# Fourier mixing and channel mix on one core: later row tables made by TensorE from the first, the sigmoid table loaded in the opening, slot 0's fold on VectorE

## The chip, the core and the metric

The kernel runs on one core of one Trainium2 chip. Five engines work from their own instruction queues: PE (TensorE, matrix products; PEld is its weight load), DVE (VectorE), ACT (ScalarE), POOL (GpSimd) and SP (SyncE, which here only issues transfers). They wait for each other by semaphores. The metric is the device time of one execution in microseconds (us), lower is better.

## The reference

The input x has 8 batches of 3072 rows and 256 columns. A two-dimensional Fourier transform is taken of each batch and its real part kept; the result goes through a channel mix with a gate:

```python
X = np.fft.fft(np.fft.fft(x, axis=1), axis=2).real
x_prev = X shifted down by one row (first row zero)
xk = mu_k * X + (1 - mu_k) * x_prev
xr = mu_r * X + (1 - mu_r) * x_prev
k = np.maximum(xk @ w_k, 0.0)          # 256 -> 1024
v = k * k @ w_v                        # 1024 -> 256
r = 1 / (1 + np.exp(-(xr @ w_r)))      # 256 -> 256
out = r * v
```

## The kernel before

**The transform in stages.** 3072 is 48 times 64, and only the real part is wanted. Each batch goes through these stages:

- *Fold* (`fold`, L171 and L173, DVE): rows of x (`xp`) plus the mirrored rows (`xm`, gathered by POOL) give `p`. A batch has two halves h, of nine and eight *slots* q. For batch 0 the folds come in parts, as the loads arrive; slot 0 of half 0 alone is folded by POOL (`fold(0, 0, 0, 1, nc.gpsimd)` within `loads`).
- *Stage A* (products with cosine and sine tables over the 48 rows, from `p` or from its sums and differences `eo`, which `butterfly` makes). Batch 0 uses `a_sum` (L592), batch 1 `a_item`, both with the table `w_pm`. Batches 2 to 7 (`a_half`, L551, and `a_slot_0`, L548) have their rows in another order: two groups of 48 rows begin at partitions 0 and 64, of 112 in all, and use the tables `w_h` and `w_h0`. `w_h0` is for slot 0 alone.
- *Stage D* (`d_units`, L614) multiplies by the tables `w_eo`, and gives `g_all`; `turned` (L637) rotates one column of each unit by a product with the table `turn`.
- *Stage C* (`c_sums`, `c_pairs`, L655) multiplies by `m_cs`; ACT and DVE evacuate the result to `y`.
- `diff`, `mix` and `mix_part` (DVE) make xk and xr from `y`.

**The channel mix.** A *chunk* is 512 rows of the output, six to a batch, 48 in all. A chunk takes four *steps*; the k products of a step (`k_products`, L766) go to a PSUM buffer of two banks, ACT makes the relu of it (L776, `rl`) and DVE the square (L786, `k`; in steps 7, 8 and 9 ACT, L784). The r products of a chunk (`r_item`, L793) go through ACT's sigmoid (L798). The v products (`v_part`, L819, in the first chunks, later `v_tile`, L807) follow some steps behind, and DVE multiplies v and r (`v_out`, L829) for the store on SP's queue.

**PSUM.** There are three buffers `psW` of two banks and two `psV` of one bank, taken in turn in the order of the program. So a product can wait for the evacuation of what lay in its buffer before.

**The tables.** In the opening the angles are products of small rows on PE; DVE wraps them, and ACT takes their sine (`w_pm` L386 and L388, `m_cs` L443, `w_eo` L487). The angles of `w_h` and `w_h0` are made by POOL (`half_rows`, L494 to L501), wrapped by DVE in step 3 (`half_tables`, L265 on `u_h`), taken through three sines by ACT (L508, L512) and scaled by DVE in step 8 (`half_scale`). The sine is in one table of functions of ACT and the sigmoid in another. ACT_TABLE_LOAD, which the compiler puts in where the function asks for it, stands ahead of the first sine (L262) and of the first sigmoid (L798, in step 5).

**The order.** All engines run in the order in which the program text issues (`pin_order`). After the opening, a loop over steps issues the k products, then the work that `at` and `event` have put down for the step: kind "x" (products with their evacuation) ahead of the step's v products, "e" (events) behind them, "w" (DVE's work) last, and then the square. In the opening, products without use (`keep_busy`, L206) fill PE's waits; `NF` holds their numbers.

**The queues.** POOL issues the loads of x, the gathers and the weights; SP issues the first load of x, the two rows of mu (L221) and all stores but three, which ACT issues at the end. The loads of batch 1 wait for a `gate` (a write by DVE, then one by POOL, L464 and L465). ACT copies mu's rows into `mu_p` (`mu_rows`, L226), which PE turns into columns (L851, `muf_t`). `zero_rows` (L423, DVE, step 3) clears rows 48 to 63 of two load buffers, which batch 2 and later don't load. `eo_rest` writes two single columns of `w_eo`, `m_first` (L450) clears one column of `m_cs`.

Of the kernel before, what the change touches and what calls it, by code (L numbers as in the profile page):

```python
# [9 lines left out]
FP32 = mybir.dt.float32  # L10
# [10 lines left out]
def _v(ap, extra_offset, free_dims):  # L21
    new_ap = [list(ap.ap[0])] + [[s, c] for (s, c) in free_dims]
    return dataclasses.replace(ap, offset=ap.offset + extra_offset, ap=new_ap)
# [16 lines left out]
def kernel(  # L40
# [98 lines left out]
    def gather(dst, src, idx):  # L139
        nc.gpsimd.indirect_dma_start(dst, None, src, bass.IndirectOffsetOnAxis(ap=idx, axis=0))  # L140
# [15 lines left out]
            load_m0(b)  # L156
        load_m(b, h, 0, 8, (idx_g8 if b > 1 else idx_8)[:, b, h:h + 1])

    def fold(b, h, q0=0, n=0, eng=None):

        n, eng = n or 9 - h, eng or V
        if (b, h) not in p_t:
            p_t[b, h] = p_pool.tile([112, 9, 256], FP16, name="p")
        k = parts(b)
        p, xp, xm = p_t[b, h][0:k], xp_t[b, h][0:k], xm_t[b, h][0:k]
        o = XM0 + 256 * (8 - h - q0)
        if (b, h, q0) == (0, 0, 0):
            xm, o = xm_00, 1
        if (b, h) == (0, 0) and q0 < 5:
            xp = xp_32  # L170
        eng.tensor_tensor(out=p[:, q0:q0 + n], in0=xp[:, q0:q0 + n],  # L171
                          in1=_v(xm, o + 256, [(-256, n), (-1, 256)]), op=ALU.add)
        eng.tensor_tensor(out=p[:, q0:q0 + n, 0], in0=xp[:, q0:q0 + n, 0],  # L173
                          in1=_v(xm, o, [(-256, n)]), op=ALU.add)

    def butterfly(b, h, n=0):
# [31 lines left out]

    fill = ps_w()
    keep_busy(4, fill)  # L210
    NF = (8, 2, 1, 3, 0, 3, 0)

# [3 lines left out]
    mu_p = const.tile([2, 2, P], FP32)  # L218
    unit = const.tile([2, 2], FP32)
    for i, mu in enumerate((moe_mu_k, moe_mu_r)):  # L220
        nc.sync.dma_start(out=mu_row[i:i + 1], in_=mu.rearrange("(a b) -> a b", a=1))  # L221

    def mu_rows(a):
        for p0, f0, step, n in (((0, 0, 1, 1), (1, 2, 2, 63), (64, 1, 2, 64)),
                                ((0, 128, 1, 1), (1, 254, -2, 63), (64, 255, -2, 64)))[a]:
            nc.scalar.activation(out=mu_p[:, a, p0:p0 + n], in_=_v(mu_row, f0, [(step, n)]),  # L226
                                 func=AF.Copy)
# [35 lines left out]
    def ts(out, in0, s1, op0, s2=None, op1=None):  # L263
        kw = {} if op1 is None else {"op1": op1}
        V.tensor_scalar(out=out, in0=in0, scalar1=s1, scalar2=s2, op0=op0, **kw)  # L265
# [46 lines left out]
    for i in range(2):  # L312
        nc.scalar.activation(out=unit[:, i:i + 1], in_=g_i[0:2], func=AF.Copy, bias=1.0 - i,
                             scale=2.0 * i - 1.0)

    ts(rv(JR, 0, (1, P)), one, 0.0, ADD)
    ts(rv(PN, 0, (2, 64), (1, 2)), _v(one, 0, [(2, 64), (0, 2)]), 0.0, ADD)
# [21 lines left out]
    WA, WB = 4 * NU, 2 * NU  # L339
    u_w = const.tile([P, 3, NU], INT32)  # L340
    w_pm = const.tile([P, 3, WA + WB], FP16)
    u_h = const.tile([P, 3, NU], INT32)
    w_h = const.tile([112, WB], FP16)
    w_h0 = const.tile([112, WB], FP16)
    u_p = const.tile([P, 2], INT32)
    u_c = const.tile([P, 2], FP32)
    u_j = const.tile([P, NU], INT32)
    ph_c = const.tile([P, 4], FP32)
    ang = (k2_pool.tile([P, 8, 512], FP16, name="rl", tag="rl")
           .rearrange("p a b -> p (a b)").bitcast(INT32)[:, 0:2 * NJ * 64]  # L350
# [37 lines left out]
        nc.scalar.activation(out=_v(w_pm, WA + g, [(WA + WB, 2), (2, NU)]),  # L388
                             in_=_v(u_w, 2 * NU, [(0, 2), (1, NU)]), **kw)

    mu_rows(0)
    mu_rows(1)

    def wrap_angles(j0, j1):
        ts(ang[:, :, j0:j1], ang[:, :, j0:j1], TURN - 1, ALU.bitwise_and)

# [23 lines left out]

    def zero_rows():
        for n in (0, 2):
            V.memset(xp_sb[n][32:64, 8], 0.0)  # L423

    def mirrored_mu():

# [4 lines left out]
    def turn_table():  # L431
        ts(turn, ramp, cols[:, 0:1], ALU.is_equal, cols[:, 1:2], MUL)
# [9 lines left out]
    def m_sine(j0, j1):  # L442
        nc.scalar.activation(out=m_cs[:, 0:2, j0:j1], in_=ang[:, :, j0:j1], func=AF.Sin,  # L443
                             bias=m_pi, scale=TWO_PI / TURN)
# [2 lines left out]
        ts(m_cs[:, 2], m_cs[:, 1], -1.0, MUL)  # L447

    def m_first():
        V.memset(_v(m_cs[hi64], 0, [(NJ * 64, 2)]), 0.0)  # L450

    def loads():
        rows()
        for a in range(2):
            gather(wk_sb[0][a], moe_w_k, row_i[:, a:a + 1])
        fold(0, 0, 0, 1, nc.gpsimd)
        nc.gpsimd.dma_start(out=wv_sb, in_=moe_w_v.rearrange("(fc p) v -> p fc v", p=128))
        half_rows()

# [13 lines left out]
    def loads_2():  # L473
        for lo in (0, 64):
            k = slice(lo, 64 if lo == 0 else 112)
            iota(idx_g8[k], pattern=[[S // 8, B], [-1, 2]], base=S // 8 - 1 - lo // 16,
                 channel_multiplier=-8)
            iota(idx_g0[k], pattern=[[S, B]], base=S - lo // 2, channel_multiplier=-64)
        iota(idx_g0[0:1], pattern=[[S, B]], base=0, channel_multiplier=0)
        for a in range(2):  # L480
            gather(wk_sb[1][a], moe_w_k, row_i[:, 2 + a:3 + a])
        load_xh(1, 1)
        for a in range(2):
            gather(wr_sb[1][a], moe_w_r, row_i[:, 2 + a:3 + a])

    def eo_sine():
        nc.scalar.activation(out=w_eo.rearrange("p a b -> p (a b)"),  # L487
# [2 lines left out]


    def half_rows():
        G = nc.gpsimd
        iota(u_j, pattern=[[1, NU]], base=0, channel_multiplier=0)  # L494
        for lo in (0, 64):
            for k in range(2):
                iota(u_p[lo:lo + 64, k:k + 1], pattern=[[0, 1]], base=k * lo // 64,
                     channel_multiplier=2)
        G.tensor_scalar(out=u_c, in0=u_p, scalar1=TURN / 96.0, scalar2=None, op0=MUL)
        for n, (k, ph) in enumerate(((0, 0.75), (0, 0.5), (1, 0.625))):  # L500
            G.tensor_scalar(out=u_h[:, n], in0=u_j, scalar1=u_c[:, k:k + 1], scalar2=ph * TURN,  # L501
                            op0=MUL, op1=ADD)

    def half_tables():
        ts(u_h, u_h, TURN - 1, ALU.bitwise_and)
        V.memset(w_h0, 0.0)
        kw = dict(func=AF.Sin, scale=TWO_PI / TURN)
        nc.scalar.activation(out=_v(w_h, 0, [(1, 2), (2, NU)]), in_=u_h[0:112, 0:2],  # L508
                             bias=m_pi[0:112], **kw)
        for g in range(2):  # L510
            rows = slice(64 * g, 64 * g + N1)
            nc.scalar.activation(out=_v(w_h0[rows], g, [(2, NU)]), in_=u_h[rows, 2],  # L512
                                 bias=m_pi[rows], **kw)
    def half_scale():
        ts(w_h0, w_h0, math.sqrt(0.5), MUL)

    def eo_rest():

        ts(w_eo[:, 0, 0:1], g_i, -1.0, MUL, 1.0, ADD)
        ts(w_eo[:, 0, 64:65], g_i, 0.0, ADD)  # L520


    a_t = {}
# [3 lines left out]
    def evac(out_ap, in_ap, eng):  # L527
        if eng == "V":
            V.tensor_copy(out=out_ap, in_=in_ap)
        else:  # L530
            nc.scalar.activation(out=out_ap, in_=in_ap, func=AF.Copy)  # L531
# [48 lines left out]
    def a_sum(b, h, i0, eng="A", m=4):  # L580


        if (h, i0) == (0, 0):
            a_tile(b)
        ps = ps_w() if m == 4 else ps_v()
        for i in range(m):
            parts = [(h, i0 + i + 1 - h, 0, 2 * WA, 0, 1)]
            if h and i0 + i == 7:
                parts = [(0, 0, 0, WA, WA, 1), (1, 7, 1, WA, 1, 2)]
            for half, q, o, n, w, step in parts:  # L590
                for k in range(2):
                    nc.tensor.matmul(out=_v(ps, 256 * i + o, [(2 * WA // n, n)]),  # L592
                                     lhsT=p_t[b, half][0:96, q, 128 * k:128 * k + 128],
                                     rhs=_v(w_pm[0:96], (WA + WB) * k + w,
                                            [(WA + WB, 2), (step, n // 2)]),
                                     start=(k == 0), stop=(k == 1))
        a_ps[b, h, i0] = ps
        if eng:
            a_evac(b, h, i0, eng, m)
# [34 lines left out]
    def turned(u0, u1, ps=None, eng="A"):  # L634
        ps = ps_w() if ps is None else ps
        f128 = _v(g_all, 256 * u0 + 128, [(256, u1 - u0)])
        nc.tensor.matmul(out=ps[:, 0:u1 - u0], lhsT=turn, rhs=f128, start=True, stop=True)  # L637
        evac(f128, ps[:, 0:u1 - u0], eng)

# [203 lines left out]
    m_sine(0, NJ1)  # L845
    eo_sine()
    m_sine(NJ1, NJ)
    fold(0, 0, 1, 4)
    mu_ps = ps_v()
    for a in range(2):  # L850
# [11 lines left out]
    fold(0, 1, 0, 4)  # L862
    a_sum(0, 1, 0, "A")
    fold(0, 1, 4, 4)
    eo_rest()
    m_first()
    turn_table()
    a_sum(0, 1, 4, "V", 2)
    a_sum(0, 1, 6, "A", 2)
    nc.scalar.activation(out=mu_n, in_=mu_f, func=AF.Copy, bias=1.0, scale=-1.0)  # L870
    m_neg()
    fill = ps_w()
# [51 lines left out]
    def at(step, f, *args):  # L924
        work.setdefault((step, "x" if f in (a_item, a_sum, d_item, d_small, c_item, c_tiles, turned, minus_0, r_item) else "w"),
                        []).append((f, args))
# [39 lines left out]
    at(0, diff, 0, 0, 4)  # L966
    at(1, d_small, 0, 12, 1)
    at(2, mix_part, 0, 1, 0, 8)
    at(3, zero_rows)
    event(3, (turned, 8, 13))  # L970
    event(4, (c_item, 0, 17, 8))
    at(4, loads_2)
    at(4, fold, 1, 0)
# [5 lines left out]
    at(7, butterfly, 1, 0, 1)  # L979
    at(7, diff, 0, 24, 26)  # L980
    at(7, mix_part, 0, 1, 8, 16)
    at(3, half_tables)
    at(8, half_scale)
    at(8, mix, 0, 0, 1, 0)
    at(9, r_item, (0, 0, 1))
    at(9, mix, 0, 0, 1, 1)
# [147 lines left out]
```

## Time and profile before

| | us |
|---|---|
| median of 3 runs | 433.0 (432.94 to 434.78) |
| the profiled execution's own time | 432.96 |
| its span, first to last instruction | 431.2 |
| PE busy in the span | 423.2 |
| DVE busy | 361.4 |
| ACT busy | 321.1 |
| POOL busy | 63.2 |

The profile is one execution with times from the span's start. "Busy" for PE is modelled and includes pipelined overlap. A timeline row gives start, length, engine, line, operation, what is written and read, and the number of instructions merged into it; brackets hold the idle time of the engine before it, and what released it. The chain is followed back from the last instruction: at each step to what released it.

### The profile page before, as it was taken

The page shows a single profiled execution, that of the slowest core. Times are in us where ns is not written, and L with a number is a line of the kernel's source. Part 1 is how long each engine was busy: PE and PEld are TensorE (multiplying, and loading weights), DVE is VectorE, ACT ScalarE, POOL GpSimd, SP SyncE. Part 2 cuts the span into 40 slices and gives each one's busy share as a digit, 9 for nine tenths or more (in the row PEclk, how much of TensorE's full clock was granted, in tenths as well). Part 3 has the DMA queues.
Part 4 walks back from the last instruction along what each step waited for, and adds up shares of the span by engine and source line. Part 5 has one row for each costly group of instructions (what it writes and reads, how often), then busy time and mean ns, then how long its engine had stood idle before and what let it go on. Part 6 is the DMA issues. An engine that isn't in the chain of part 4 may idle for free.

```text
span 431.2 us, 9311 instructions
## 1 busy us (share of the span) xinstructions
PE 423.2 (98%) x3853; PEld 298.2 (69%) x3853; DVE 361.4 (84%) x552; ACT 321.1 (74%) x375; POOL 63.2 (15%) x100
## 2 busy tenths in 40 slices
PE   8999999999999999999999999999999999999996
PEld 3656776777767776777677777777676766766765
DVE  8899989997998979988898988989799847997453
ACT  7799798877778678777877777777786867666661
POOL 7785402000050001400041000500000000000000
PEclk9999999999999999999999999999999999999999
DMA  8999926323286223943259223772232322223233
GB/s 170 137 150 208 220 54 111 82 60 75 52 145 152 69 69 62 184 104 75 49 106 192 70 50 74 131 162 63 62 75 49 75 62 63 65 65 72 69 74 98
DMA packets 35102, 42.06 MB, mean 98 GB/s; under 512 B 4114, under 2 KB 31092, under 8 KB 35060
## 3 DMA queue, kind: packets, MB, share of 16 engines
q1 hardware_dynamic: 27492, 25.41, 23.8%
q0 software_dynamic: 7264, 15.80, 22.3%
q8 instruction: 30, 0.49, 0.5%
q10 hardware_dynamic: 304, 0.26, 0.2%
q14 instruction: 12, 0.10, 0.1%
HBM read 32.08 MB, written 25.17 MB: 133 GB/s over the span
## 4 chain that ended last, share of the span: by engine, by line
PE 93%; DVE 5%; ACT 1%; issue 0%; POOL 0%; ACTq 0%
PE psW L766 38%; PE psV L807 36%; PE psW L793 10%; PE psW L614 2%; PE psV L819 2%; PE psW L687 1%; PE psW L574 1%; DVE p L171 1%; DVE rl L265 1%; PE psW L655 1%; ACT rl L776 0%; DVE k L786 0%; PE psW L592 0%; DVE x L731 0%; DVE d L708 0%
## 5 line engine op out<-in xcount | busy, mean ns | idle before, releaser
L776 ACT ACTIVATE rl<-psW 128x1024 f16<-128x1024 f32 x192 | 195.2, 1025 | 91.1 <-PE psW L766 87.4
L766 PE MATMUL psW<-x,wk 128*128 128x512 f16 (+1 forms) x776 | 195.7, 377 | 0.7 <-ACT r L798 0.2
L807 PE MATMUL psV<-wv_sb,k 128*128 128x256 f16 x1424 | 184.1, 273 | 0.0
L807 PEld LDWEIGHTS <-k 128*128 128x128 f16 x1424 | 137.0, 98 | 35.7
L786 DVE TENSOR_TENSOR k<-rl 128x2048 f16<-128x2048 f16 (+1 forms) x101 | 116.3, 1152 | 33.3 <-ACT rl L776 32.9
L766 PEld LDWEIGHTS <-wk 128*128 128x128 f16 x776 | 74.9, 98 | 53.9 <-issue 1.6
L829 DVE SCALAR_TENSOR_TENSOR o<-psV,r 128x512 f32<-128x512 f32 (+1 forms) x97 | 65.9, 682 | 15.4 <-PE psV L807 13.4
L731 DVE TENSOR_TENSOR x<-y,t 128x1536 f16<-128x1536 f16 (+2 forms) x72 | 61.6, 861 | 2.1
L793 PE MATMUL psW<-wr,x 128*128 128x256 f16 x384 | 49.8, 273 | 0.5 <-ACT rl L776 0.5
L798 ACT ACTIVATE r<-psW 128x1024 f16<-128x1024 f32 x48 | 48.9, 1019 | 0.8 <-PE psW L793 0.8
L793 PEld LDWEIGHTS <-x 128*128 128x128 f16 x384 | 37.5, 98 | 15.0 <-DVE p L171 0.8
L465 POOL IOTA gate<- 1x1 int32 x6 | 2.1, 356 | 198.8 <-DVE gate L464 198.8
L531 ACT ACTIVATE a<-psW 128x832 f16<-128x832 f32 x31 | 26.1, 863 | 2.6 <-PE psW L574 1.4
L531 ACT ACTIVATE g_all<-psW 128x1024 f16<-128x1024 f32 (+5 forms) x37 | 25.6, 695 | 0.4 <-PE psW L637 0.2
L140 POOL DMA_INDIRECT xm<-in_x_dram,idx_g x18 | 23.8, 1320 | 5.5 <-issue 5.5
L171 DVE TENSOR_TENSOR p<-xp,xm 112x2304 f16<-112x2304 f16 (+5 forms) x18 | 21.3, 1181 | 0.0
L720 DVE TENSOR_SCALAR t<-d,muf_t 128x1536 f16<-128x1536 f16 (+2 forms) x40 | 20.8, 530 | 0.0
L720 DVE TENSOR_SCALAR t<-d,mu_m 128x1536 f16<-128x1536 f16 x32 | 19.7, 615 | 0.0
L614 PEld LDWEIGHTS <-a 128*128 128x128 f16 x208 | 14.0, 98 | 6.5 <-ACT a L531 0.5
L182 DVE TENSOR_TENSOR eo<-p 112x1152 f16<-112x1152 f16 (+3 forms) x28 | 17.9, 680 | 0.0
L531 ACT ACTIVATE pq<-psW 128x1024 f16<-128x1024 f32 (+1 forms) x18 | 15.2, 879 | 2.3 <-PE psW L687 2.3
L708 DVE TENSOR_TENSOR d<-y 128x1664 f16<-128x1664 f16 (+5 forms) x19 | 16.7, 880 | 0.2 <-ACT y L531 0.2
(141 smaller groups left out, 218.7 us busy)
## 6 DMA issues: line engine op xcount, KB each, us to landing
out_dram<-o SPq DMA_DIRECT2D x189, 128.0 KB, 2.4
xp<-in_x_dram POOLq DMA_DIRECT2D x12, 216.0 KB, 4.4
xp<-in_x_dram POOLq DMA_DIRECT2D x13, 192.0 KB, 7.6
xp<-in_x_dram POOLq DMA_DIRECT2D x2, 384.0 KB, 6.3
wv_sb<-in_moe_w_v_dram POOLq DMA_DIRECT2D x1, 512.0 KB, 9.0
xp<-in_x_dram SPq DMA_DIRECT2D x1, 480.0 KB
xp<-in_x_dram POOLq DMA_DIRECT2D x1, 432.0 KB, 6.8
xm<-in_x_dram,idx_g POOLq DMA_INDIRECT x18, 8.1
```

What stands on the lines that cost most here:

```text
L140: nc.gpsimd.indirect_dma_start(dst, None, src, bass.IndirectOffsetOnAxis(ap=idx, axis=0))
L171: eng.tensor_tensor(out=p[:, q0:q0 + n], in0=xp[:, q0:q0 + n], in1=_v(xm, o + 256, [(-256, n), (-1, 256)]), op=ALU.add)
L531: nc.scalar.activation(out=out_ap, in_=in_ap, func=AF.Copy)
L720: V.tensor_scalar(out=dst, in0=src, scalar1=mu, scalar2=None, op0=ALU.mult)
L731: V.tensor_tensor(out=_v(x_t[b, j, m], o, [(64 * step, hi - lo), (step, 64)]), in0=y_t[b][:, lo + 3 * m:hi + 3 * m, a], in1=x_t["t", a][:, ...
L766: nc.tensor.matmul(out=st["k", ds][:, 512 * hs + lo:512 * hs + hi], lhsT=wk_sb[m][a][:, 128 * fc:128 * fc + 128], rhs=xk[:, a, 512 * i + l ...
L776: nc.scalar.activation(out=st["rl"][:, 2 * ds:2 * ds + 2], in_=st["k", ds].rearrange("p (f t) -> p f t", f=2), func=AF.Relu, bias=0.0, sca ...
L786: V.tensor_tensor(out=k2_t[c][:, lo:hi], in0=r, in1=r, op=ALU.mult)
L793: nc.tensor.matmul(out=ps[:, 256 * tb:256 * tb + 256], lhsT=x_t[b, 1, m][:, a, 512 * i + 128 * tb: 512 * i + 128 * tb + 128], rhs=wr_sb[m] ...
L798: nc.scalar.activation(out=st["r", c], in_=ps, func=AF.Sigmoid)
L807: nc.tensor.matmul(out=st["v", tb - h][:, 256 * h:256 * h + 256], lhsT=k2_t[c][:, fc, 128 * tb:128 * tb + 128], rhs=wv_sb[:, fc], start=(f ...
L829: V.scalar_tensor_tensor(out=o.rearrange("p a b -> p (a b)")[:, 0:256 * n], in0=st["v", t0][:, 0:256 * n], scalar=16.0, in1=st["r", c][:, ...
```

## The change

Seven parts:

1. *The later tables.* POOL's angles, DVE's wrap, ACT's three sines and DVE's clearing and scaling go. POOL makes a table `order` of ones and zeros (an iota and a comparison). In step 3, behind `turned(8, 13)` and in the same PSUM buffer, three products of `order` with columns of `w_pm` put the finished first tables' rows into the later order; one DVE copy of 112 x 104 brings `w_h` and `w_h0`, now one tile, from PSUM. `turned`'s own evacuation stays on ACT.
2. *The sigmoid.* A sigmoid of one column of zeros follows the last sine of the opening, so that the table load stands there, ahead of stage A's first evacuation.
3. *Slot 0's fold* of batch 0 goes from POOL to DVE, behind `fold(0, 1, 4, 4)` and ahead of DVE's evacuation `a_sum(0, 1, 4, "V", 2)`.
4. *Small writes.* `eo_rest` and `m_first` go from DVE to POOL, into `loads`, where the fold was. `turn_table` comes behind the two `a_sum`, so DVE does it after its evacuation.
5. *mu.* Its two loads are issued by ACT, ahead of the Sine table's load. The copies into `mu_p` come ahead of the sines of `w_pm`.
6. `zero_rows` goes from DVE in step 3 to POOL, at the end of `loads_2`, behind the last `wr` gather and ahead of batch 2's loads.
7. `NF[1]`, the filling products ahead of the first `a_sum`, is 4 and was 2.

```diff
-    def fold(b, h, q0=0, n=0, eng=None):
+    def fold(b, h, q0=0, n=0):
...
-        eng.tensor_tensor(out=p[:, q0:q0 + n], in0=xp[:, q0:q0 + n],
-                          in1=_v(xm, o + 256, [(-256, n), (-1, 256)]), op=ALU.add)
+        V.tensor_tensor(out=p[:, q0:q0 + n], in0=xp[:, q0:q0 + n],
+                        in1=_v(xm, o + 256, [(-256, n), (-1, 256)]), op=ALU.add)
...
-    NF = (8, 2, 1, 3, 0, 3, 0)
+    NF = (8, 4, 1, 3, 0, 3, 0)
...
-        nc.sync.dma_start(out=mu_row[i:i + 1], in_=mu.rearrange("(a b) -> a b", a=1))
+        nc.scalar.dma_start(out=mu_row[i:i + 1], in_=mu.rearrange("(a b) -> a b", a=1))
...
+    mu_rows(0)
+    mu_rows(1)
...
-    w_h = const.tile([112, WB], FP16)
-    w_h0 = const.tile([112, WB], FP16)
+    w_hh = const.tile([112, 2 * WB], FP16)
+    w_h, w_h0 = w_hh[:, 0:WB], w_hh[:, WB:2 * WB]
+    order_i = const.tile([P, P], INT32)
+    order = const.tile([P, P], FP16)
...
-    mu_rows(0)
-    mu_rows(1)
-
...
     def zero_rows():
         for n in (0, 2):
-            V.memset(xp_sb[n][32:64, 8], 0.0)
+            nc.gpsimd.memset(xp_sb[n][32:64, 8], 0.0)
...
     def m_first():
-        V.memset(_v(m_cs[hi64], 0, [(NJ * 64, 2)]), 0.0)
+        nc.gpsimd.memset(_v(m_cs[hi64], 0, [(NJ * 64, 2)]), 0.0)
...
     def loads():
         rows()
         for a in range(2):
             gather(wk_sb[0][a], moe_w_k, row_i[:, a:a + 1])
-        fold(0, 0, 0, 1, nc.gpsimd)
+        eo_rest()
+        m_first()
         nc.gpsimd.dma_start(out=wv_sb, in_=moe_w_v.rearrange("(fc p) v -> p fc v", p=128))
         half_rows()
...
             gather(wr_sb[1][a], moe_w_r, row_i[:, 2 + a:3 + a])
+        zero_rows()
...
     def half_rows():
+        iota(order_i, pattern=[[1, 2], [2, 64]], base=0, channel_multiplier=-1)
+        nc.gpsimd.tensor_scalar(out=order, in0=order_i, scalar1=0.0, scalar2=None,
+                                op0=ALU.is_equal)
+
+    def half_tables():
+        ps = ps_w()
+        turned(8, 13, ps, "")
+        for o, w, step in ((512, 0, 2), (512, 1, 2), (512 + WB, WA, 1)):
+            nc.tensor.matmul(out=ps[0:112, o:o + WB], lhsT=order[0:96, 0:112],
+                             rhs=_v(w_pm[0:96], w, [(step, WB)]), start=w != 1, stop=w > 0)
+        evac(_v(g_all, 256 * 8 + 128, [(256, 5)]), ps[:, 0:5], "A")
+        V.tensor_copy(out=w_hh, in_=ps[0:112, 512:512 + 2 * WB])
+
+    def eo_rest():
+
         G = nc.gpsimd
-        iota(u_j, pattern=[[1, NU]], base=0, channel_multiplier=0)
-        for lo in (0, 64):
-            for k in range(2):
-                iota(u_p[lo:lo + 64, k:k + 1], pattern=[[0, 1]], base=k * lo // 64,
-                     channel_multiplier=2)
-        G.tensor_scalar(out=u_c, in0=u_p, scalar1=TURN / 96.0, scalar2=None, op0=MUL)
-        for n, (k, ph) in enumerate(((0, 0.75), (0, 0.5), (1, 0.625))):
-            G.tensor_scalar(out=u_h[:, n], in0=u_j, scalar1=u_c[:, k:k + 1], scalar2=ph * TURN,
-                            op0=MUL, op1=ADD)
-
-    def half_tables():
-        ts(u_h, u_h, TURN - 1, ALU.bitwise_and)
-        V.memset(w_h0, 0.0)
-        kw = dict(func=AF.Sin, scale=TWO_PI / TURN)
-        nc.scalar.activation(out=_v(w_h, 0, [(1, 2), (2, NU)]), in_=u_h[0:112, 0:2],
-                             bias=m_pi[0:112], **kw)
-        for g in range(2):
-            rows = slice(64 * g, 64 * g + N1)
-            nc.scalar.activation(out=_v(w_h0[rows], g, [(2, NU)]), in_=u_h[rows, 2],
-                                 bias=m_pi[rows], **kw)
-    def half_scale():
-        ts(w_h0, w_h0, math.sqrt(0.5), MUL)
-
-    def eo_rest():
-
-        ts(w_eo[:, 0, 0:1], g_i, -1.0, MUL, 1.0, ADD)
-        ts(w_eo[:, 0, 64:65], g_i, 0.0, ADD)
+        G.tensor_scalar(out=w_eo[:, 0, 0:1], in0=g_i, scalar1=-1.0, scalar2=1.0, op0=MUL, op1=ADD)
+        G.tensor_scalar(out=w_eo[:, 0, 64:65], in0=g_i, scalar1=0.0, scalar2=None, op0=ADD)
...
     m_sine(NJ1, NJ)
+    nc.scalar.activation(out=warm, in_=zeros[:, 0:1], func=AF.Sigmoid)
...
     fold(0, 1, 4, 4)
-    eo_rest()
-    m_first()
-    turn_table()
+    fold(0, 0, 0, 1)
     a_sum(0, 1, 4, "V", 2)
     a_sum(0, 1, 6, "A", 2)
+    turn_table()
...
-    at(3, zero_rows)
-    event(3, (turned, 8, 13))
+    event(3, (half_tables,))
...
-    at(3, half_tables)
-    at(8, half_scale)
```

More of the change, by code (lines that the diff above doesn't have):

```diff
@@ L157, in load_xh @@
         load_m(b, h, 0, 8, (idx_g8 if b > 1 else idx_8)[:, b, h:h + 1])
-    def fold(b, h, q0=0, n=0, eng=None):
-        n, eng = n or 9 - h, eng or V
+    def fold(b, h, q0=0, n=0):
+        n = n or 9 - h
         if (b, h) not in p_t:
@@ L170, in fold @@
             xp = xp_32
-        eng.tensor_tensor(out=p[:, q0:q0 + n], in0=xp[:, q0:q0 + n],
-                          in1=_v(xm, o + 256, [(-256, n), (-1, 256)]), op=ALU.add)
-        eng.tensor_tensor(out=p[:, q0:q0 + n, 0], in0=xp[:, q0:q0 + n, 0],
+        V.tensor_tensor(out=p[:, q0:q0 + n], in0=xp[:, q0:q0 + n],
+                        in1=_v(xm, o + 256, [(-256, n), (-1, 256)]), op=ALU.add)
+        V.tensor_tensor(out=p[:, q0:q0 + n, 0], in0=xp[:, q0:q0 + n, 0],
                           in1=_v(xm, o, [(-256, n)]), op=ALU.add)
@@ L341 @@
     w_pm = const.tile([P, 3, WA + WB], FP16)
-    u_h = const.tile([P, 3, NU], INT32)
-    w_h = const.tile([112, WB], FP16)
-    w_h0 = const.tile([112, WB], FP16)
-    u_p = const.tile([P, 2], INT32)
-    u_c = const.tile([P, 2], FP32)
-    u_j = const.tile([P, NU], INT32)
+    w_hh = const.tile([112, 2 * WB], FP16)
+    w_h, w_h0 = w_hh[:, 0:WB], w_hh[:, WB:2 * WB]
+    order_i = const.tile([P, P], INT32)
+    order = const.tile([P, P], FP16)
     ph_c = const.tile([P, 4], FP32)
@@ L637, in turned @@
         nc.tensor.matmul(out=ps[:, 0:u1 - u0], lhsT=turn, rhs=f128, start=True, stop=True)
-        evac(f128, ps[:, 0:u1 - u0], eng)
+        if eng:
+            evac(f128, ps[:, 0:u1 - u0], eng)
     def c_slots(s0, n):
```

## The prediction

> **What bounds the kernel now.** I read the page's busy shares and chain first, then the stretches of the opening, PE's waits, the chain in order of time and the timeline. The page:
>
> ```profile
> span 431.2 us, 9311 instructions
> PE 423.2 (98%) x3853; PEld 298.2 (69%) x3853; DVE 361.4 (84%) x552; ACT 321.1 (74%) x375; POOL 63.2 (15%) x100
> ...
> PE 93%; DVE 5%; ACT 1%; issue 0%; POOL 0%; ACTq 0%
> ```
>
> The execution is PE from end to end but for about 26 us of DVE and ACT on the chain (6% of 431.2). Two stretches (busy columns PE, PEld, DVE, ACT, POOL) show where that is:
>
> ```profile
> 25.00:30.00 5.00, 4.48 (x46) 2.71 (x45) 4.63 (x12) 3.97 (x8) 4.08 (x5) 1.00 0.71 105
> ...
> 35.00:40.00 5.00, 5.00 (x37) 3.51 (x36) 4.93 (x13) 4.97 (x6) 3.55 (x4) 1.00 1.09 207
> ```
>
> From 35 us PE is never free, and the granted clock is 1.00 in both. So the change can move the end only by what it takes out of the opening, up to about 35 us; later work only moves along. PE's own waits, and the chain (start, length, engine, tile, line):
>
> ```profile
> PE psW L592 <- DVE p L173: 1.0, 1, 1.0
> ...
> PE psW L793 <- ACT rl L776: 0.5, 1, 0.5
> PE psV L592 <- DVE p L173: 0.4, 1, 0.4
> PE psW L766 <- ACT r L798: 0.2, 1, 0.2
> ```
>
> ```profile
> 26.10 0.30 DVE xp L423 x2
> 26.43 0.19 DVE u_h L265
> ...
> 26.92 0.32 ACT w_h L512
> ...
> 27.59 1.03 ACT rl L776
> ...
> 31.78 1.01 ACT r L798
> ...
> 34.76 0.86 PE psW L766 x4
> ...
> 47.81 0.09 PE psW L548 x2
> ```
>
> This chain passes straight through what is removed: zeroed rows (L423), the angle wrap of the later tables (L265 u_h), their sines (L512), and a sigmoid held up by its table load. At 34.76 PE has just finished the step-7 value products, and from there on it is busy, as the second stretch shows. So I ask when that 34.76 comes in the changed kernel.
>
> **The opening, 0 to 15 us.** Timeline rows (start, length, engine, line; in brackets the idle time before and its releaser):
>
> ```profile
> 1.56 0.22 SPq L221 DMA_DIRECT2D mu_row<-in_moe_mu_r_dram  x1
> ...
> 4.35 0.63 ACT L386 ACTIVATE w_pm<-u_w,sc 128x104 f16<-128x104 int32 x1 [1.07 <-DVE ph_c L265]
> ...
> 5.74 0.87 ACT L226 ACTIVATE mu_p<-mu_row 2x1 f32<-2x1 f32 x6
> ...
> 6.52 1.23 ACT L399 ACTIVATE rl<-psV,ph_c 128x512 int32<-128x512 f32 x2
> ...
> 8.78 1.21 DVE L171 TENSOR_TENSOR p<-xp,xm 96x1024 f16<-96x1024 f32 x1
> 8.89 1.15 ACT L443 ACTIVATE m_cs<-rl,sc 128x1024 f16<-128x1024 int32 x1
> ...
> 11.18 2.61 ACT L531 ACTIVATE a<-psW 128x832 f16<-128x832 f32 x3 [1.14 <-PE psW L592]
> ...
> 11.71 0.17 DVE L173 TENSOR_TENSOR p<-xp,xm 96x4 f16<-96x4 f16 x1
> ...
> 12.52 0.70 DVE L173 TENSOR_TENSOR p<-xp,xm 96x4 f16<-96x4 f16 x1
> 12.53 0.64 POOL L171 TENSOR_TENSOR p<-xp,xm 96x256 f16<-96x256 f32 x1
> ...
> 13.26 0.19 POOL L173 TENSOR_TENSOR p<-xp,xm 96x1 f16<-96x1 f32 x1
> ...
> 13.28 1.07 PE L592 MATMUL psV<-w_pm,p 96*128 96x208 f16 x10 [0.39 <-DVE p L173]
> ...
> 14.38 0.55 ACT L531 ACTIVATE a<-psV 128x416 f16<-128x416 f32 x1 [0.59 <-PE psV L592]
> ...
> 14.98 0.90 PEld L614 LDWEIGHTS <-a 128*128 128x128 f16 x16 [0.48 <-ACT a L531]
> ```
>
> *Fold on VectorE.* The same little DVE instruction takes 0.17 at 11.71 and 0.70 at 12.52, where POOL's fold runs beside it: 0.53 lost. Without it DVE is free at 12.69, does slot 0 itself (a quarter of the 1.21 row, 0.30, to the 0.42 of a 256-column copy quoted below, plus 0.17) and ends at about 13.2. PE's ten products no longer stand behind it: they start at 12.75, not 13.28, and only the last four read slot 0. PE would have them at about 13.85, 0.5 earlier. DVE also loses two 1-column writes and a memset to POOL (L265, L450). The data of slot 0 is there by then, as POOL's fold of it started at 12.53.
>
> *Sigmoid table.* The other end of this stage is ACT, which loses its idle 1.14. The last sine ends at 10.04 as before (DVE's angles release it). The load is 1.28 (row below) and the dummy sigmoid an estimated 0.2 (the one-column row on POOL), so the evacuations start at about 11.5, not 11.18: three take 2.61 (to 14.1), the fourth 0.55: 14.66 against 14.93. So ACT, not PE, now sets this point, and of the 0.5 only **0.27** is left. The two extra filling products fit in PE's wait of 1.0 for the first fold and cost nothing; if that cover were gone, 0.43 (512 columns are a quarter of the 0.86 on the chain).
>
> A rule speaks against this term. The Trainium skill, "ScalarE: Activation LUTs", What ACT_TABLE_LOAD costs, adds a drain of about 1380 ns to a load of 1283 ns. The sum would then lose 1.38 here. The trace agrees with the 1283 and shows no drain: the sigmoid is on the chain from 31.78, and the load ended at 30.47 + 1.28 = 31.75.
>
> *mu rows by ACT's queue.* The two issues leave SP, where nothing waited for them, and stand ahead of ACT's Sine load. An issue is 0.22 on SP for 1 KB, and 0.55 to 0.74 on ACT for stores:
>
> ```profile
> L837 ACTq DMA_DIRECT2D out_dram<-o x3: 552/685/742, 426.0 to 427.6; - x3
> ```
>
> The copies of mu (0.78 from 5.74 to 6.52) move ahead of the first tables too. ACT has 1.07 free before 4.35; 0.44 + 0.78 makes it 0.15 late, 1.48 + 0.78 makes it 1.2 late. From 4.35 to the last sine at 8.89 ACT runs without a gap, of which 0.78 is now gone: so 0.78 of lateness is free, and the ends are 0 and 0.4. I take 0, as the size of the transfer is that of the SP row. The data must have landed: in the old order it had by 5.74, with an issue half a microsecond later. Up to a landing at 4.35 the wait costs nothing, beyond it one for one. Taken: no cost. The shortest and median landings of stores, 2.3 and 2.4, put it near 3.5.
>
> ```profile
> DMA to landing us min/median/max: 2.3/2.4/10.3
> ...
> out_dram<-o SPq DMA_DIRECT2D x4, 128.0 KB, 7.4
> ```
>
> *POOL's queue.* The fold's 0.83 goes, three tiny writes come (0.2 each by the 0.19 row): the value weights' load behind them leaves 0.2 earlier. Nine small instructions for the old angles become an iota and one comparison of 128 columns; POOL then waits for the gate, as before, which covers both. The two memsets moved to POOL stand ahead of batch 2's loads and delay those by two DVE memsets' 0.30, or twice that; batch 2 is folded at step 17, thirteen steps later, and that slack covers it. Against the gain: POOL's tiny writes now fall at 12.5 to 13.0, beside DVE's fold, and its comparison beside DVE's negation of the sine table. By the 0.53 lost in 0.64 of POOL work, 0.6 of POOL could hold DVE for up to 0.5; that reaches the end only past the 0.46 by which ACT is later than PE's products would be. Ends 0 to 0.3, taken 0.
>
> **Steps 3 to 7, 24 to 35 us.**
>
> ```profile
> 15.42 0.42 DVE L529 CAST g_all<-psV 128x256 f16<-128x256 f32 x1 [0.68 <-PE psV L614]
> ...
> 26.67 0.36 ACT L508 ACTIVATE w_h<-u_h,sc 112x52 f16<-112x52 int32 x1 [0.99 <-DVE w_h L506]
> ...
> 27.16 1.35 DVE L171 TENSOR_TENSOR p<-xp,xm 96x2304 f16<-96x2304 f16 x1
> ...
> 29.57 0.69 DVE L708 TENSOR_TENSOR d<-y 128x1024 f16<-128x1024 f16 x1 [0.22 <-ACT y L531]
> ...
> 30.47 1.28 ACT L798 ACT_TABLE_LOAD   x1
> ...
> 32.82 1.29 DVE L829 SCALAR_TENSOR_TENSOR o<-psV,r 128x512 f32<-128x512 f32 x2 [0.43 <-ACT r L798]
> ```
>
> *PE* gets three products of 52 columns. Two such cost 0.09 on the chain, so 0.14, or twice that if each weight load shows. They come at 24.5, on the path for the next two microseconds; after that PE waits for DVE anyway.
>
> *ACT* loses three sines (0.36 + 2 x 0.32), the 0.99 that it waited for DVE's wrap before them, and the load of 1.28. The relu of 27.59 can start when its products are done, about 25.9; the step-5 relevance products lose their 0.5 wait, and the sigmoid that ended at 32.78 ends near 30.3. By ACT alone PE would come 1.2 earlier to step 7.
>
> *DVE* decides instead, because between 26 and 34 it has only two short waits. It loses 0.30 + 0.19 and a memset between them (another 0.06 or so, L506) and gets one copy of 104 columns from PSUM (0.17 for a tiny instruction, 0.42 for 256 columns: 0.27), net 0.3. Its two waits on ACT, 0.22 and 0.43, go as well. So the output multiply of 32.82 comes at about 31.9, 0.3 + 0.22 + 0.43 = 0.95 earlier, if PE's value products are done by then (about 31.9 by the same reckoning). These free the bank into which step 7's products go; PE reaches 34.76 about **0.9** earlier, with ends of 0.5 (the loads bind the fold of 27.16, or POOL's work does) and 1.2 (DVE does not bind). What is late next is that DVE multiply. The scaling of the odd table, at step 8, stood beside a busy PE and gives nothing.
>
> **The sum.** 0.27 + 0.9 = 1.2 off the span. Its execution took 432.96 (431.2 and 1.76 around it), practically the median of 433.0. So 431.8, 0.28% less.
>
> **Rivals.**
>
> *The opening pays for the table (432.6).* If the switch costs ACT more than 1.55, or POOL's small work holds DVE, the opening's 0.27 turns into a loss. With a switch of twice its row (2.56) that loss is 1.0 and the time 433.0 - 0.9 + 1.0 = 433.1; half way, 432.6. For it: ACT becomes the last one in that stage. Against: the 1.28 row. By the drain of the Trainium skill's page above, the loss would be 1.11 and the time 433.2; the row speaks against it.
>
> *Slower: mu lands late.* ACT now waits for mu ahead of every table. A landing L after 4.35 delays the last sine, and all behind it, one for one; at L = 5.55 it has eaten the 1.2. With the 7.4 of stores in the busy stretch after 30 us, L would be 8.6 and the time 431.8 + 4.25 = 436.0. For it: the first loads of x share the DMA engines. Against: in the old order a landing by 5.74 was in time, after an issue at 1.56; the earlier issue puts L at 5.3 or less, and the total at 432.8 or less.
>
> *PE follows ACT (431.3).* If DVE does not bind, nor ACT the opening, 0.5 + 1.2 = 1.7 comes back. For it: PE's two waits of 0.5 and 0.2 are for ACT. Against: DVE's row of 32.82.
>
> *Nothing shows (432.8).* If the stages swap waits without reaching PE, because the fold of 27.16 waits for its load or the new copy waits for ACT.
>
> **Chances and range.** About 0.5% (2.2 us) is what a measurement of this kernel can tell from no change. Forecast (431.3 to 432.3): 0.57. Opening pays: 0.15, within 0.5%. PE follows ACT, or more: 0.15, of which 0.07 falls below 430.8. Nothing shows: 0.06. mu late: 0.07, of which 0.06 beyond 435.2. Hence faster 0.07, same 0.87, slower 0.06. The range of 8 in 10 runs from 430.9 to 433.1; the forecast's own is 431.3 to 432.3.
>
> **What would show it.** DVE's small fold row back at 0.17 and PE's products at about 12.75; a table load at 10.05 and the evacuations from 11.5; the d products' weights at about 14.7; no w_h rows; the relevance products of step 5 without a wait; the output multiply at about 31.6 with the opening's shift; PE without a gap from about 33.6. A wait of ACT before the mu copies, a POOL row under a long DVE row between 12.5 and 15, or a DVE fold waiting for its load near 26.5 would make it wrong.

## The result, and the profile after

| | before | after |
|---|---|---|
| median of 12 runs, us | 433.77 (432.94 to 434.78) | 432.09 (431.46 to 433.47) |
| profiled execution, us | 432.96 | 432.30 |
| its span, us | 431.2 | 430.5 |

The ratio is 0.9965, with a 95% interval of 0.9954 to 0.9977: 0.35% less time, where 0.28% was forecast. Executions of one kernel lie in two groups here, some 1.1 to 2 us apart (e8 to e11 below take up why), and medians and ratios take in both, while the quoted profile of before is from the lower group of its kernel (near 433.05; the other lies near 434.2). So the two profiles, 0.7 apart, show less than the medians do.

The page of the changed kernel, with its busy shares and its chain:

```profile
span 430.5 us, 9306 instructions
PE 422.7 (98%) x3858; PEld 298.3 (69%) x3858; DVE 360.8 (84%) x547; ACT 320.3 (74%) x373; POOL 62.7 (15%) x96
...
PE 89%; DVE 4%; DMA 3%; ACT 3%; issue 0%; ACTq 0%; SPq 0%; DVEq 0%
```

DMA has come onto the chain with 3%. Two transfers make it up: a load of mu at the start and a store of the output. The waits of PE in the changed kernel:

```profile
PE psW L582 <- DVE p L173: 1.3, 1, 1.3
PE psW L206 <- DVE xm L234: 1.0, 1, 1.0
PE psV L810 <- DVE o L820: 0.6, 1, 0.6
```

The three waits that the prediction quoted for steps 5 to 7 and for slot 0's fold are gone; a new one of 0.6, for DVE's output multiply, has come. The opening in the timeline (columns as before):

```profile
4.67 0.89 ACT L226 ACTIVATE mu_p<-mu_row 2x1 f32<-2x1 f32 x6 [1.05 <-DMA mu_row<-in_moe_mu_r_dram]
...
9.20 1.13 ACT L440 ACTIVATE m_cs<-rl,sc 128x1024 f16<-128x1024 int32 x1
...
10.35 1.28 ACT L839 ACT_TABLE_LOAD   x1
...
11.76 2.35 ACT L521 ACTIVATE a<-psW 128x832 f16<-128x832 f32 x3
...
12.54 0.23 DVE L173 TENSOR_TENSOR p<-xp,xm 96x4 f16<-96x4 f16 x1
...
12.82 1.07 PE L582 MATMUL psV<-w_pm,p 96*128 96x208 f16 x10
...
14.60 0.90 PEld L604 LDWEIGHTS <-a 128*128 128x128 f16 x16 [0.56 <-ACT a L521]
```

DVE's small fold is back at 0.23, PE's ten products start at 12.82 instead of 13.28, and stage D's weights at 14.60 instead of 14.98. But ACT waits 1.05 for mu, and its last sine starts at 9.20, 0.31 later than before. Steps 5 to 12:

```profile
27.80 1.02 ACT L767 ACTIVATE rl<-psW 128x1024 f16<-128x1024 f32 x1
28.73 1.02 ACT L789 ACTIVATE r<-psW 128x1024 f16<-128x1024 f32 x1
...
31.25 1.29 DVE L820 SCALAR_TENSOR_TENSOR o<-psV,r 128x512 f32<-128x512 f32 x2
...
33.15 1.03 PE L757 MATMUL psW<-x,wk 128*128 128x512 f16 x4
...
39.06 0.69 DVE L820 SCALAR_TENSOR_TENSOR o<-psV,r 128x512 f32<-128x512 f32 x1
...
41.24 0.69 DVE L820 SCALAR_TENSOR_TENSOR o<-psV,r 128x512 f32<-128x512 f32 x1 [1.48 <-DMA out_dram<-o]
...
41.99 0.60 PE L810 MATMUL psV<-wv_sb,k 128*128 128x256 f16 x4 [0.57 <-DVE o L820]
```

The sigmoid follows the relu without a table load, the output multiply comes at 31.25 instead of 32.82, and step 8's k products at 33.15. In the kernel before the same row stood at 34.59:

```profile
34.59 1.03 PE L766 MATMUL psW<-x,wk 128*128 128x512 f16 x4
```

So PE was 1.44 ahead at 33 us. At 41.24 the output multiply waits 1.48 for a store. The chain, in order of time, shows which store, and two of its later rows show what is left. The first two rows are of the changed kernel; the last two are batch 1's 32 stage C products, in the changed kernel and in the kernel before:

```profile
32.74 8.38 DMA out_dram<-o
...
58.09 1.00 PE psW L646 x32
```

```profile
58.80 1.00 PE psW L655 x32
```

The store issued at 32.7 took 8.38 to land, and its buffer, one of three, was needed again at 39.8. Of the 1.44, 0.71 is left at 58 us, and that is the difference of the two spans: from this row to the end both need 372.4.

### The profile page after: what moved, and what is told of

The parts are those of the page before. It is cut to its first block, busy times and chain, and to the rows that moved or that the text cites. A ratio compares the mean times of both kernels' runs of the same rounds, so it can differ in the third digit from the quotient of the medians.

```text
span 430.5 us, 9306 instructions
## 1 busy us (share of the span) xinstructions
PE 422.7 (98%) x3858; PEld 298.3 (69%) x3858; DVE 360.8 (84%) x547; ACT 320.3 (74%) x373; POOL 62.7 (15%) x96
## 4 chain that ended last, share of the span: by engine, by line
PE 89%; DVE 4%; DMA 3%; ACT 3%; issue 0%; ACTq 0%; SPq 0%; DVEq 0%
PE psV L798 36%; PE psW L757 36%; PE psW L784 9%; PE psW L604 2%; DMA out_dram<-o 2%; PE psW L678 1%; PE psW L564 1%; PE psV L810 1%; DVE k L777 1%; DMA mu_row<-in_moe_mu_r_dram 1%; ACT a L521 1%; DVE o L820 1%; PE psW L646 0%; DVE x L722 0%; DVE d L699 0%; ACT m_cs L440 0%
## 5 line engine op out<-in xcount | busy, mean ns | idle before, releaser
L171 DVE TENSOR_TENSOR p<-xp,xm 112x2304 f16<-112x2304 f16 (+6 forms) x19 | 21.6, 1139 | 0.0
## 6 DMA issues: line engine op xcount, KB each, us to landing
xp<-in_x_dram POOLq DMA_DIRECT2D x1, 432.0 KB, 5.5
```

## The experiments

Three positions describe each profile: the start of stage D's weights (opening), of the first output multiply (steps 3 to 7), and of batch 1's 32 stage C products (all). Ratios are to the kernel before.

| kernel | D's weights | output | C products | ratio (95%) |
|---|---|---|---|---|
| before | 14.98 | 32.82 | 58.80 | |
| after | 14.60 | 31.25 | 58.09 | 0.9965 (0.9954, 0.9977) |
| e1, after, four output buffers | 15.04 | 31.76 | 57.86 | 0.9956 (0.9943, 0.9968) |
| e2, after, sigmoid table late | 14.49 | 31.19 | 58.43 | 0.9972 (0.9958, 0.9986) |
| e3, before, only the tables by TensorE | 15.01 | 32.10 | 58.07 | 0.9971 (0.9960, 0.9983) |
| e5, after, mu as before | 14.48 | 31.60 | 57.57 | 0.9974 (0.9961, 0.9987) |
| e6, e5 with four buffers | 14.50 | 31.89 | 57.88 | 0.9967 (0.9956, 0.9979) |
| e7, before, four buffers | 14.98 | 32.93 | 58.92 | 0.9990 (0.9979, 1.0000) |
| e8, e6 with the table late | 16.11 | 33.44 | 59.43 | 0.9963 (0.9950, 0.9976) |
| e9, e6 with the fold on POOL | 15.01 | 32.22 | 58.19 | 0.9978 (0.9968, 0.9987) |
| e10, e6 with 8 fillings | 14.55 | 31.29 | 57.36 | 0.9952 (0.9939, 0.9965) |
| e11, e6 with 2 fillings | 14.55 | 31.29 | 57.39 | 0.9961 (0.9948, 0.9973) |
| e12, after again | 15.11 | 31.76 | 58.66 | 0.9963 (0.9950, 0.9977) |
| e13, e10 again | 14.49 | 31.39 | 57.35 | 0.9952 (0.9938, 0.9965) |

The intervals overlap in most pairs: the positions separate the causes, the ratios only the largest sums.

### The new wait: e1 and e7

```diff
-                        bufs=3 if n == 2 else 1)
+                        bufs=4 if n == 2 else 1)
```

> The changed kernel with four output buffers of v times r where it has three. Theory W (a new wait gives part of the gain back: at 41.24 us DVE waits 1.48 for the store of 32.74, because the third output buffer is not yet free, and PE loses 0.57 to 0.7): the wait is gone, PE keeps all of the 1.4 us that it has gained by 33 us, the step products of 59.1 us come 0.6 to 0.7 earlier, and the ratio to the kernel before falls from 0.9965 to about 0.995. Rival D (the loads fill the DMA engines there, and whatever waits for them only shifts): the wait shows up at the next output or at a fold, and the ratio stays at 0.9965.

> The kernel before with four output buffers where it has three. Theory W: the kernel before has no such wait (its second output follows the first at 40.63 without idle time), so the fourth buffer is worth nothing: ratio 0.999 to 1.001. Rival D2 (the buffers are short in both, in executions that the one profile does not show): ratio 0.998 or less, and the gain of the fourth buffer says nothing on the change.

In e1's profile the wait for the store is gone: both output multiplies follow each other.

```profile
39.57 1.29 DVE L820 SCALAR_TENSOR_TENSOR o<-psV,r 128x512 f32<-128x512 f32 x2
```

Its opening was 0.44 slower than that of the changed kernel (mu, below), and yet its C products came 0.23 earlier: 0.67 of the loss is back, as theory W said. One profile without a wait would prove little, since e5 has three buffers and no such wait either. But of the five profiles with the new tables and three buffers four show it (after, e2, e3 and e12), and of the seven with four buffers none. The time fell less than the profile suggests, to a median of 431.94 against 432.09, a difference that these runs do not tell from noise; the wait is not in each execution. e7 is the control: without the change the fourth buffer gives 0.999, with 1.000 at the end of the interval, and its positions are within 0.12 of those of before. So the fewness of the buffers comes to light when the work ahead of them gets faster. In e12 it showed at a later output and with an even longer wait:

```profile
51.97 0.69 DVE L820 SCALAR_TENSOR_TENSOR o<-psV,r 128x512 f32<-128x512 f32 x1 [1.64 <-DMA out_dram<-o]
```

### The table load: e2

```diff
-    nc.scalar.activation(out=warm, in_=zeros[:, 0:1], func=AF.Sigmoid)
```

> The changed kernel without the dummy sigmoid, so that the table load stands ahead of the first real sigmoid, in step 5, again. Theory S (without the three sines ACT has room for the load in step 5, and DVE decides there): the opening gets 0.2 to 0.4 shorter (D's weights at 14.2 to 14.4 instead of 14.60), the sigmoid comes 1.28 later, to about 31, just ahead of the output multiply of 31.25; ratio 0.995 to 0.997, as the changed kernel or a little better. Rival T (the load in step 5 was what held PE): the output multiply and PE come 0.6 to 1.3 later, ratio 0.998 to 0.999.

The load stands in step 5 again, and the output multiply behind it is not late. ACT and DVE rows of e2:

```profile
28.79 1.28 ACT L789 ACT_TABLE_LOAD   x1
30.08 1.02 ACT L789 ACTIVATE r<-psW 128x1024 f16<-128x1024 f32 x1
```

```profile
31.14 0.05 issue
31.19 1.29 DVE o L820 x2
```

The sigmoid ends at 31.10, just in time for a DVE that could not have come earlier, as it was at work until 31.14. The opening is only 0.11 shorter than in the changed kernel, not the 0.2 to 0.4 expected. For the rest theory S holds: the early load neither gained nor cost anything that a measurement tells. That its C products stand at 58.43 is the store again (a wait of 1.98 at 51.74).

### The tables alone: e3

```diff
-    event(3, (turned, 8, 13))
+    event(3, (half_tables,))
...
-    at(3, half_tables)
-    at(8, half_scale)
```

and `half_rows` and `half_tables` as in the changed kernel; all else is the kernel before.

> The kernel before with only the first part of the change: the later tables by TensorE from the first. The sigmoid's table load stays in step 5, slot 0's fold on POOL, the zeroed rows on DVE. Theory of the sum's second term (sines and wrap gone from ACT, DVE decides): the opening as before (14.98), the relevance products of step 5 without their 0.5 wait, DVE's output multiply 0.4 to 0.6 earlier than 32.82 by its two waits on ACT that go; ratio about 0.9987. Rival (that gain is the sigmoid's alone): ratio 1.000.

The opening is as it was (15.01), step 5's relevance products have lost their wait, and the output multiply comes at 32.10: 0.72 earlier, more than the 0.4 to 0.6 expected. The C products keep this to the end of the stage, 0.73, although the sigmoid's load still stands in step 5 and the zeroed rows on DVE. This is in spite of two waits of the output multiply for a store (0.72 at 41.20 and 0.61 at 51.15). A ratio of 0.9971, where 0.9987 was expected, is most of the change's gain from this part alone. What the move of `zero_rows` gives was not tried alone.

### mu: e5 and e6

```diff
-        nc.scalar.dma_start(out=mu_row[i:i + 1], in_=mu.rearrange("(a b) -> a b", a=1))
+        nc.sync.dma_start(out=mu_row[i:i + 1], in_=mu.rearrange("(a b) -> a b", a=1))
```

and `mu_rows` behind the sines of `w_pm` again; e6 has the fourth buffer as well.

> The changed kernel with only mu as before, and its three output buffers. Theory M with W: the opening is 0.1 to 0.2 shorter than in the changed kernel, but DVE's wait for the store near 41 us gets longer by as much, since the landing of the store does not move: D's weights at 14.4 to 14.5, ratio 0.9965 as the changed kernel. Rival (the wait moves with the work): ratio 0.9960 or less.

> The changed kernel with four output buffers, and with mu as before (loads on SP's queue, copies behind the sines of the first tables). Theory M (mu's landing, at 4.57 and 5.04 us in two profiles of the new order, holds ACT and costs the opening 0.2 to 0.7): the last sine starts at 8.9, D's weights at 14.4 to 14.5, and with no wait for a store the step products of 59.1 us stand at about 57.3; ratio about 0.995, the best of all. Rival (ACT's lateness was covered): D's weights at 14.6 or later, as in the changed kernel.

The last sine starts at 8.92 in e5, and D's weights at 14.48 and 14.50. In the three profiles with the new order and the early table load the copies of mu started at 4.67, 5.11 (e1) and 4.59 (e12), in each case behind a wait, and D's weights came at 14.60, 15.04 and 15.11. e12 had a late load of x as well (DVE's third fold waited 0.48 for it), so its 15.11 is not mu's alone. Against e5's 14.48 mu's new place so cost the opening 0.12 in one profile and 0.56 in another. It costs this beside the early table load: in e2, which has the new order without it, the copies started at 4.49 and D's weights still came at 14.49. For the rest the expectations failed: e5's profile has no wait for a store, and e6 did not reach 57.3, as its output multiply waited 0.63 for PE's value products although PE's rows before it look as in the changed kernel. ACT was let go late there too: its relu of the products of 29.69 started at 31.76, in the changed kernel that of 29.68 at 30.74. Why stays open. Three of e5's twelve runs and two of e6's were near 433.6, which the next experiments take up.

### Slot 0's fold: e9

```diff
-        eo_rest()
-        m_first()
+        fold(0, 0, 0, 1, nc.gpsimd)
...
-    fold(0, 0, 0, 1)
     a_sum(0, 1, 4, "V", 2)
```

and the small writes and the turn table where they were before, on DVE, ahead of `a_sum`.

> As e6_four_mu, with slot 0's fold on POOL again and the small writes on DVE, where they were (the late sines, the wrap and the zeroed rows stay gone). Theory of the opening's term (POOL's fold holds DVE's small fold for 0.5): DVE's small fold at 12.5 takes 0.7 instead of 0.2, D's weights come at about 14.9 instead of 14.4 to 14.5, all behind it 0.4 to 0.5 later, ratio 0.001 higher. Rival (ACT alone sets the stage, as it has the table load): D's weights within 0.15 of e6_four_mu.

```profile
12.60 0.65 DVE L173 TENSOR_TENSOR p<-xp,xm 96x4 f16<-96x4 f16 x1
```

The small fold takes 0.65 again, and D's weights start at 15.01, 0.51 later than in e6. The ratio is 0.0011 higher, and the C products come 0.31 later than e6's, which had lost time at the wait above. This part, the fold with the small writes, is worth half a microsecond in the opening, if nothing else is late. In the SBUF page of the Trainium skill ("SBUF — State Buffer", in its table of terms) the port pair that DVE and GpSimd share is an exclusive lock for a whole instruction. The 0.65 and 0.70 beside POOL's fold of 0.64, and 0.17 to 0.23 without it, agree with that.

### An idle PE and its clock: e8, e10, e11

> As e6_four_mu, and without the dummy sigmoid, so that the table load stands in step 5. Theory S (ACT has room in step 5 once the three sines are gone): D's weights and the output multiply as in e6_four_mu within 0.2, ratio equal to it within 0.001. Rival T (the load in step 5 holds PE): the output multiply 0.6 to 1.3 later than in e6_four_mu.

e8 is e6 without the dummy sigmoid. Its profiled execution was the longest of its five runs (433.67, the others 431.72 to 432.16), and its stretches show why. The columns are the stretch, busy PE, PEld, DVE, ACT and POOL, then the granted clock:

```profile
8.00:10.00 2.00, 0.62 (x3) 0.10 (x1) 1.97 (x4) 2.00 (x3) 1.68 (x7) 1.00 1.05 201
10.00:12.00 2.00, 1.72 (x15) 1.48 (x16) 1.90 (x8) 0.86 (x2) 1.59 (x2) 0.85 0.85 138
12.00:14.00 2.00, 2.00 (x13) 1.51 (x11) 1.17 (x4) 0.93 (x2) 1.77 (x5) 0.50 0.97 140
14.00:16.00 2.00, 2.00 (x15) 1.39 (x12) 1.07 (x3) 1.36 (x3) 1.23 (x3) 0.79 0.75 113
```

PE had done its fillings by 8.6, stood idle for 1.66 until the first fold, and got half its clock from about 11.4 to 14.8 (0.85, 0.50 and 0.79 as means of half and full rate); D's weights came at 16.11, not within 0.2 of e6's as expected. From there the output multiply was 17.3 later, in e6 17.4. In both it waited some 0.6 for PE's value products, and in e8 the sigmoid had ended at 33.06, 0.38 ahead of it: on the table load e8 says the same as e2. In e10 and e11 the fillings ahead of the first stage A product are the only edit to e6, eight in e10 and two in e11. For e10:

```diff
-    NF = (8, 4, 1, 3, 0, 3, 0)
+    NF = (8, 8, 1, 3, 0, 3, 0)
```

> As e6_four_mu, with eight filling products ahead of the first stage A product where it has four. Theory C (the executions that are 1.1 to 2 us longer are those in which PE stands idle for some 1.7 us before 10.28 and its granted clock then falls to 0.5, as in the profile of e8_four_mu_siglate): the gap before 10.28 is 0.8 or less, no execution comes near 433.6, and the median is 431.6 to 431.9. Where PE reaches its full rate late, the fillings run past 10.28 and may cost up to 0.6. Rival (the longer executions have nothing to do with the gap): one execution in six is again near 433.6.

> As e6_four_mu, with two filling products there, as in the kernel before. Theory C: the gap is 0.43 longer than in e6_four_mu where PE has its full rate early, so at least as many executions are near 433.6 as there (2 of 12), and those without the fall of the clock are as fast (431.5). Rival: no more long executions than with eight fillings.

With eight, all six runs lay between 431.46 and 431.98; PE's only wait in the profile is the one at the very start:

```profile
PE psW L206 <- DVE xm L234: 1.0, 1, 1.0
```

With two, three of twelve runs lay at 433.0 to 433.2 and the others at 431.3 to 431.9. Both agree with theory C, though six and twelve runs could differ so by chance, and 57.36 is the position that e6 should have had. The clock's fall itself was seen in one profile only, but each run has a mean granted clock on record, and 3.4 us at half rate in 430 would make it 0.996. Of the 106 runs of kernels with the new tables, 18 have 0.996 or less and took 433.03 or more; the 88 others took 432.92 or less. So a lower clock makes up this upper group. It goes with the fillings: 34 of 117 executions of kernels with two (before, e3, e7, e11), 11 of 71 with four and none of 11 with eight. These kernels differ in other things too, and in the profiles gaps of 0.9 to 1.4 stood without a fall, so that the gap alone brings it about is likely and not shown.

### The best version beside the changed kernel: e12 and e13

> The changed kernel as it is, once more, on the chip of the next run. Theory (mu's landing and the wait for the store hold it in many executions, the fall of the clock in some): median 432.0 to 432.3, and its profile shows at least one of a last sine after 9.1 and an output waiting for a store near 41.

> The kernel of e10_four_mu_fill8 once more, beside the changed kernel: if its four output buffers, mu in its old place and eight fillings are worth what the profiles show, its median lies 0.4 to 0.6 below that of the run before it, near 431.6, with no execution near 433.5. Rival: the two medians within 0.2.

On the same chip the changed kernel's median was 432.08 (431.57 to 432.87) and that of e10's kernel 431.49 (431.39 to 431.68), 0.59 less, against 433.62 for the kernel before. The expected signs were there: the last sine of e12 starts at 9.13, though its output waits for a store near 52 and not near 41, and no run of e13 is near 433.5. Four output buffers, mu in its old place and eight fillings so lie clearly below the kernel before (0.9952, twice) and below the changed kernel on one chip with five runs each; the intervals of the two ratios overlap. The eight fillings do not lower the median (e11 with two has 431.53); none of their eleven runs is a long one.

## Why the prediction was right, and where not

- *The sum.* 1.2 us was forecast; the medians moved by 1.7 and the ratio's interval, times 433.8, is 1.0 to 2.0. The two profiles moved by 0.7. Part of the 1.7 is probably the clock: a mean of 0.996 or less stands on record for 25 of the 81 executions of the kernel before that ran beside the experiments, and for 1 of 17 of the changed kernel; without these the medians are 433.3 and 432.0, 1.3 apart. The prediction priced the two extra filling products at nothing; that they may spare falls of the clock it did not ask. That the sum came so near is partly luck: the mechanism of the largest term was right, but three others were off, in both directions (the opening, mu and the wait for a store).
- *The opening, 0.27.* Measured 0.38 (14.98 to 14.60), by errors that offset each other. The fold's part was right: the small fold, PE's start (12.75 forecast, 12.82 found) and, by e9, 0.5 in all. But ACT's sine did not end at 10.04 "as before": mu landed late. And the three evacuations took 2.35, not 2.61, as they no longer waited for PE within the group; this hid mu's cost. "So ACT, not PE, now sets this point" held in the changed kernel only because of mu. With mu in its old place (e5) the three evacuations are done by 13.84, the fourth starts at 13.88, as in e2 without a table load ahead, and the opening gains the fold's whole 0.50:

```profile
11.49 2.35 ACT L521 ACTIVATE a<-psW 128x832 f16<-128x832 f32 x3
...
13.88 0.55 ACT L521 ACTIVATE a<-psV 128x416 f16<-128x416 f32 x1
...
14.48 0.90 PEld L604 LDWEIGHTS <-a 128*128 128x128 f16 x16 [0.48 <-ACT a L521]
```

- *mu, no cost.* This step failed. The landing was put near 3.5 from the shortest and the median store. It was 4.57 by the chain (3.26 after the second issue at 1.31), with the loads of x in flight, and about 5.0 in e1. The rival's mechanism was there: from its threshold of 4.35 on the last sine came later one for one, by 0.31 and in e1 by 0.75. What lay behind it did not: D's weights came 0.12 and 0.56 after e5's, 0.19 less in both. The landing stayed below the rival's 5.55, and within the bound of 5.3. The sign that the prediction named for it, a wait of ACT before the mu copies, came with 1.05.
- *The sigmoid's table.* The load took 1.28 without a drain, ahead of the 0.20 of the dummy sigmoid. By the figure of the Trainium skill, "ScalarE: Activation LUTs", What ACT_TABLE_LOAD costs, the stage would have ended 1.38 later; neither this trace nor e2's shows that. What the prediction did not ask is whether the load needed to move. Once the sines are gone, step 5 has room for it (e2), and in the opening it stands in a stage that ACT ends when mu is late.
- *Steps 3 to 7, 0.9.* Measured 1.06: 1.44 at step 8's k products less 0.38 from the opening. That DVE decides was right, also in e2, where ACT was 1.3 later and the output multiply was not. The copy of 104 columns cost 0.26 (0.27 forecast) and the three products on PE 0.17 by the chain of e6 (0.14 forecast):

```profile
24.23 0.17 PE psW L500 x3
```

- *"PE without a gap from about 33.6"* was wrong. The prediction let all later work move along with PE, and did not look at what is paced by transfers, though it had the stores' 7.4 in hand for mu. An output buffer comes free when its store lands, and the stores issued between 30 and 45 us landed after 6.1 to 10.2 (median 8.4), while batch 2's loads kept the DMA engines busy. That took 0.73 back in the profiled execution, 0.67 of it by e1.
- *Rivals.* "PE follows ACT" did not come about, "Nothing shows" neither; "The opening pays" describes what e1 and e12 show at D's weights (15.04 and 15.11), but its cause, a dearer table load or POOL's work, is not theirs: mu was late in both, and in e12 a load of x.

## What to carry to other kernels

When a stage gets faster, list every buffer behind it that a transfer must free, with the landing time of that transfer in its own stretch, not the median over the kernel: a buffer count that was just enough becomes the next wait. A tiny load is not a fast load when it shares the DMA engines with big ones (1 KB took 3.26 us here), so whatever waits for it belongs late in the order of its engine. Before a table load or a fill is moved, look where its old place has slack after the other edits. And before medians are compared, look at the granted clock of each run: up to 0.4 of the 1.7 us here may come from fewer falls of it.

## What was not expected of the hardware

- The first products of the opening run at half rate, though the granted clock is listed as 1.00 there: the first four of 512 columns took 1.89, as long as eight later ones in the profile of after. For how long differs between executions: the same eight took 2.38 in the profile of before and 2.79 in e2's. Where PE is at full rate early it has a longer gap ahead, and some 1.1 us after a gap of 1.66 the granted clock fell to 0.50 for some 3.4 us (e8), which brought D's weights 1.6 later than in e6. The Trainium skill, "TensorE: Matmul & The Clock Gate", Part 1, tells of a free-running window of about 3.4 us and of a default at half rate. The length agrees. The rule of the Trainium skill, "TensorE: Matmul & The Clock Gate", Why this matters for your kernels, to keep gaps below about 3 us would have allowed this gap.
- A load of 1 KB took 3.26 us to land beside the loads of x, and stores of 128 KB 8.4 and 11.3, against a median of 2.4 over the whole kernel before.
